# The second MLP's first product as seven block products, with weights' parts kept in HBM

## The chip, the cores and the metric

The kernel runs on one core of a Trainium2 chip. The metric is the device time of one execution in microseconds. Three runs of the kernel before gave 929.76, 930.53 and 929.92 us, so the median is 929.92. Profiles come from one profiled execution; its span runs from the first to the last instruction.

## The reference

Attention with random features over 4 batches, 8 heads, 576 tokens and head size 64 makes 2304 tokens of 512 values. Two MLPs follow, both 512 to 2048 to 512. All is float32.

```
attention: num = phi(q) (phi(k)^T v),  den = phi(q) sum(phi(k)),  x = num / (den + 1e-6)
first MLP:  h = x @ w_in;  g = max(h, 0) + alpha * min(h, 0);                       x = g @ w_out
second MLP: h = x @ w_in;  g = h if h >= 1, 0 if h <= -1, else (h + 1)^2 / 4;       out = g @ w_out
```

## The kernel before

**Split products.** To keep float32 precision each factor is split into a rounded part hi and a rest lo, and a product is three matmuls that add up in one PSUM bank (`mm3`, L257 to L260): hi hi, hi lo and lo hi. ScalarE makes hi (`hi_of`, L242, in some places VectorE), VectorE or GpSimd makes lo by a subtraction (`lo_of`, L250 to L253).

**Units.** The tokens stand in five blocks: four of 512 tokens (one of each batch) and one of 256 (the last 64 tokens of each). They form four groups, the last of which has a 512 and the 256 block. The 2048 features stand in 16 pieces of 128. A unit is one MLP, one group and one piece, so there are 2 x 4 x 16 = 128 units, and `mlps` (L813) runs them in order: h of the next unit (4 chunks of 128 input values, 3 matmuls each), then the second product of the unit before. h goes to one of two PSUM banks (h0, h1). `activate` turns it into g_hi and g_lo, and only then is the bank free. The second product adds into banks y0 to y3, a0 and a1 over all 16 pieces of a group. In the second MLP its result has the tokens on the partitions and goes straight to the output.

**Weights.** They arrive as 64-bit numbers; `convert` loads 128x1024 words (raw) and makes 128x512 float32 of them with two operations of ScalarE (or one of GpSimd), two of VectorE and one addition of GpSimd (L293). The converted weights of an MLP stay in SBUF. Each unit splits its two 128x512 pieces anew (`split_weight`: w_hi on ScalarE, w_lo on GpSimd), so every piece is split four times, once for each group.

**What sets the order.** All is written by a planner: each piece of work is a generator that asks for an engine and a time, a token (a buffer) or an event. `Plan.run` always takes the operation that can start first by its own table of costs (on a tie the one with the lower rank; `URGENT` is -10). So the order of each engine is fixed when the program is built, and the engines wait for each other by semaphores. All loads and stores are issued by SyncE's queue in that order. Attention is spread over the first three groups of the first MLP; when it ends (event "late"), the second MLP's weights are loaded.

Of the kernel before, what the change touches and what calls it, by code (L numbers as in the profile page):

```python
# [161 lines left out]
def favor_attention_two_mlps(  # L162
# [20 lines left out]
    nc = tc.nc  # L183
# [13 lines left out]
    NE = NF // 2  # L197
# [3 lines left out]
    WARM = 18  # L201
    COLS_NS = 1260
# [4 lines left out]
    wpool = ctx.enter_context(tc.tile_pool(name="w", bufs=NF))  # L207
# [5 lines left out]
    psum = ctx.enter_context(tc.tile_pool(name="psum", bufs=1, space=PSUM))  # L213

# [42 lines left out]
    def mm3(out_, wh, wl, mh, ml, first, last):  # L257
        nc.tensor.matmul(out_, wh, mh, start=first, stop=False)  # L258
        nc.tensor.matmul(out_, wh, ml, start=False, stop=False)  # L259
        nc.tensor.matmul(out_, wl, mh, start=False, stop=last)  # L260
# [39 lines left out]
    def load_weights(l, src):  # L300
        for f in range(NF):
            if l == 0:
                yield ev("unit", f - AHEAD)
            if l == 1 and f < NE:
                yield ev("late")
                w = late["pool"].tile([P, 2, DM], F32, tag="w", name="w2", bufs=NE)
            else:
                yield w_slots
                w = wpool.tile([P, 2, DM], F32, tag="w", name="w")
            weights[l, f] = w  # L310
            for a in range(2):
                i = l * len(groups) * NF + f
                plan.add(convert(w[:, a, :], src[f, :, a * 2 * DM : (a + 1) * 2 * DM], (l, f, a)), weight_rank(i))
# [4 lines left out]
    def split_weights(a):  # L318
        for i, (l, g, f) in enumerate(units):
            yield part_slots[a]  # L320
            yield ev("w", l, f, a)
            hi = parts_p.tile([P, DM], F32R, tag=f"wh{a}", name="w_hi")
            lo = parts_p.tile([P, DM], F32R, tag=f"wl{a}", name="w_lo")
            parts[i, a] = hi, lo
            plan.add(split_weight(a, i, weights[l, f][:, a, :], hi, lo), weight_rank(i) - 0.1)

    def split_weight(a, i, w, hi, lo):
# [4 lines left out]
        if l == 0 and g == len(groups) - 1:  # L332
            if ev("split", f).at is not None:
                plan.put(w_slots, 0)
            done("split", f)
# [348 lines left out]
    def attended():  # L684
# [6 lines left out]
        late["pool"] = ctx.enter_context(tc.tile_pool(name="late", bufs=1, reuse_waits="tile"))  # L691
# [10 lines left out]
    def split_x(l, b, c):  # L702
        n = sizes[b]
        k = b // B
        yield ev("x", l, b)
# [8 lines left out]
        done("xs", l, b, c)  # L714
# [5 lines left out]
    def activate(i, b, h, tag):  # L720
        l, _, f = units[i]
# [4 lines left out]
        if l == 0:  # L726
            a = alpha_sb[:, f : f + 1]
            yield _dve(n, lambda: nc.vector.tensor_scalar(tn, hn, 0.0, a, ALU.min, ALU.mult))  # L728
            yield _dve(n, lambda: nc.vector.scalar_tensor_tensor(hn, hn, 0.0, tn, ALU.max, ALU.add))
        else:  # L730

            yield _dve(n, lambda: nc.vector.tensor_scalar(tn, hn, -1.0, 1.0, ALU.max, ALU.min))  # L732
            yield _act(n, lambda: nc.scalar.activation(tn, tn, AF.Square, bias=half[:, 0:1], scale=0.5), 50)  # L733
            yield _dve(n, lambda: nc.vector.tensor_tensor(hn, hn, tn, ALU.max))  # L734
# [3 lines left out]
        g_hi = pool.tile([P, n], F32R, tag=f"gh{k}", name="g_hi", bufs=2)  # L738
        g_lo = pool.tile([P, n], F32R, tag=f"gl{k}", name="g_lo", bufs=2)
# [18 lines left out]
    def project(i, b, c, y):  # L758
        l, _, f = units[i]
# [5 lines left out]
        if l == 1:  # L765
            return _pe(mm3_ns(DM), lambda: mm3(y, gh[:, cc], gl[:, cc], hi, lo, first, last))
# [13 lines left out]
    def finish(l, b, c, y, tag, tokens):  # L780
        n = sizes[b]
        if l == 0:
# [12 lines left out]
        if l == 0:  # L795
            done("y", b, c)
            return
# [191 lines left out]
```

## Time and profile before

| | before |
|---|---|
| median of 3 runs | 929.92 us |
| span of the profiled execution | 928.7 us |
| TensorE busy | 914.9 us |
| VectorE, ScalarE, GpSimd busy | 543.0, 508.4, 456.0 us |
| moved by DMA | 53.41 MB |
| end of attention | about 321 us |
| second MLP's first matmul | about 526 us |
| last matmul starts | 923.3 us |

In the profile PE is TensorE's matmuls, PEld its weight loads, DVE VectorE, ACT ScalarE, POOL GpSimd, SP SyncE. Busy matmuls overlap: each has a latency behind its columns. How fast they follow each other is read from their starts.

### The profile page before, as it was taken

What the parts mean: (1) busy time and instruction counts of PE and PEld (TensorE: products, weight loads), DVE (VectorE), ACT (ScalarE), POOL (GpSimd) and SP (SyncE); (2) the same over time, 40 slices, a digit from 0 to 9 for tenths busy, and PEclk for the clock granted to TensorE, in tenths of its full rate; (3) what the DMA queues carried; (4) which work ended last, traced back from release to release, by engine and by line L of the source; (5) the groups of instructions that cost most, each with busy time, mean ns of one, the idle gap of its engine ahead of it and who ended that gap; (6) DMA issues with size and microseconds to landing.
All of it is one profiled execution on the core that took longest, in us unless ns stands there. A gap on an engine that the chain in (4) does not pass through costs nothing.

```text
span 928.7 us, 14192 instructions
## 1 busy us (share of the span) xinstructions
PE 914.9 (99%) x5244; PEld 759.3 (82%) x5244; DVE 543.0 (58%) x942; ACT 508.4 (55%) x1052; POOL 456.0 (49%) x375
## 2 busy tenths in 40 slices
PE   8899999999999999999999999999999999999997
PEld 7677887788888888888888888888888888888886
DVE  6988798866666678786544533353335355443332
ACT  7887777655556465665522544464445445443343
POOL 3656667543344477776643254444444444333330
PEclk9999999999999999999999999999999999999999
DMA  8654444111120022243200000010001000100002
GB/s 253 201 168 137 141 163 130 39 40 39 56 75 1 1 91 91 91 137 137 91 1 1 1 1 1 1 46 1 1 1 46 0 1 1 46 1 1 1 1 68
DMA packets 33861, 53.41 MB, mean 58 GB/s; under 512 B 20992, under 2 KB 21120, under 8 KB 33792
## 3 DMA queue, kind: packets, MB, share of 16 engines
q1 hardware_dynamic: 33712, 52.48, 17.6%
q8 instruction: 41, 0.67, 0.3%
q14 instruction: 28, 0.23, 0.1%
q10 hardware_dynamic: 80, 0.03, 0.0%
HBM read 47.78 MB, written 4.72 MB: 57 GB/s over the span
## 4 chain that ended last, share of the span: by engine, by line
PE 89%; DVE 5%; ACT 2%; DMA 1%; SPq 1%; issue 1%; POOL 0%; ACTq 0%; DVEq 0%
PE h L258 14%; PE h L260 13%; PE h L259 13%; PE y L258 12%; PE y L259 12%; PE y L260 12%; PE a L258 2%; PE a L260 2%; PE a L259 2%; PE a L394 2%; DMA raw<-w 1%; DVE x_lo L252 1%; PE a L431 1%; PE a L489 1%; DVE nm L361 1%
## 5 line engine op out<-in xcount | busy, mean ns | idle before, releaser
L253 POOL TENSOR_TENSOR w_lo<-w,w_hi 128x512 fp32r<-128x512 f32 x256 | 336.6, 1316 | 387.8 <-ACT w_hi L242 382.0
L242 ACT ACTIVATE w_hi<-w 128x512 fp32r<-128x512 f32 x256 | 161.7, 632 | 188.1 <-PE h L259 132.9
L258 PE MATMUL h<-x_hi,w_hi 128*128 128x512 f32 (+1 forms) x640 | 239.3, 374 | 0.0
L260 PE MATMUL h<-x_hi,w_lo 128*128 128x512 f32 (+1 forms) x640 | 236.0, 369 | 0.2 <-POOL w_lo L253 0.2
L259 PE MATMUL h<-x_lo,w_hi 128*128 128x512 f32 (+1 forms) x640 | 236.0, 369 | 0.0
L258 PEld LDWEIGHTS h<-x_hi,w_hi 128*128 128x128 f32 x640 | 120.7, 189 | 22.1 <-DVE g_lo L251 0.8
L260 PEld LDWEIGHTS h<-x_hi,w_lo 128*128 128x128 f32 x640 | 120.5, 188 | 21.2 <-POOL w_lo L253 0.7
L242 ACT ACTIVATE g_hi<-h 128x512 fp32r<-128x512 f32 (+1 forms) x160 | 88.8, 556 | 89.2 <-DVE h L734 46.7
L259 PEld LDWEIGHTS h<-x_lo,w_hi 128*128 128x128 f32 x640 | 120.7, 189 | 19.2
L251 DVE TENSOR_TENSOR g_lo<-h,g_hi 128x512 fp32r<-128x512 f32 (+1 forms) x160 | 100.6, 635 | 53.4 <-ACT g_hi L242 51.0
L732 DVE TENSOR_SCALAR t<-h 128x512 f32<-128x512 f32 x80 | 51.0, 637 | 131.6 <-PE h L260 129.9
L728 DVE TENSOR_SCALAR t<-h,alpha_sb 128x512 f32<-128x512 f32 x80 | 55.5, 694 | 87.9 <-PE h L260 86.7
L293 POOL TENSOR_TENSOR w<-w,raw 128x512 uint32<-128x512 uint32 x64 | 88.5, 1390 | 32.2 <-DVE w L292 26.5
L258 PE MATMUL y<-g_hi,w_hi 128*128 128x512 f32 x256 | 104.1, 407 | 0.0
L259 PE MATMUL y<-g_lo,w_hi 128*128 128x512 f32 x256 | 100.2, 391 | 0.0
L260 PE MATMUL y<-g_hi,w_lo 128*128 128x512 f32 x256 | 100.1, 391 | 0.0
L258 PE MATMUL y<-w_hi,g_hi 128*128 128x512 f32 x256 | 99.8, 390 | 0.0
L259 PE MATMUL y<-w_lo,g_hi 128*128 128x512 f32 x256 | 99.8, 390 | 0.0
L260 PE MATMUL y<-w_hi,g_lo 128*128 128x512 f32 x256 | 99.6, 389 | 0.0
L733 ACT ACTIVATE t<-t,half 128x512 f32<-128x512 f32 x80 | 54.5, 681 | 59.6 <-DVE t L732 59.6
L734 DVE TENSOR_TENSOR h<-h,t 128x512 f32<-128x512 f32 x80 | 51.4, 643 | 49.3 <-ACT t L733 49.3
L260 PEld LDWEIGHTS y<-g_hi,w_lo 128*128 128x128 f32 x256 | 48.1, 188 | 10.7
(121 smaller groups left out, 1262.6 us busy)
## 6 DMA issues: line engine op xcount, KB each, us to landing
raw<-w SPq DMA_DIRECT2D x64, 512.0 KB, 3.9
kq<-kq SPq DMA_DIRECT2D x15, 576.0 KB, 5.0
vm<-v SPq DMA_DIRECT2D x16, 256.0 KB, 3.6
out<-x SPq DMA_DIRECT2D x16, 256.0 KB, 2.0
vl<-v SPq DMA_DIRECT2D x32, 16.0 KB, 3.2
out<-x SPq DMA_DIRECT2D x4, 128.0 KB, 2.3
kq<-kq SPq DMA_DIRECT2D x1, 320.0 KB, 3.5
kq<-kq SPq DMA_DIRECT2D x1, 256.0 KB, 3.2
```

The lines of the kernel that those rows point to most:

```text
L242: ops = [_act(n, lambda: nc.scalar.activation(hi, src, AF.Copy))]
L251: "dve": _dve(n, lambda: nc.vector.tensor_tensor(*args), bias),
L253: "pool": _pool(n, lambda: nc.gpsimd.tensor_tensor(*args)),
L258: nc.tensor.matmul(out_, wh, mh, start=first, stop=False)
L259: nc.tensor.matmul(out_, wh, ml, start=False, stop=False)
L260: nc.tensor.matmul(out_, wl, mh, start=False, stop=last)
L293: yield _pool(n, lambda: nc.gpsimd.tensor_tensor(d, d, low, ALU.add))
L394: nc.tensor.matmul(o, x[rows, c], om[rows, :], start=True, stop=True)
L728: yield _dve(n, lambda: nc.vector.tensor_scalar(tn, hn, 0.0, a, ALU.min, ALU.mult))
L732: yield _dve(n, lambda: nc.vector.tensor_scalar(tn, hn, -1.0, 1.0, ALU.max, ALU.min))
L733: yield _act(n, lambda: nc.scalar.activation(tn, tn, AF.Square, bias=half[:, 0:1], scale=0.5), 50)
L734: yield _dve(n, lambda: nc.vector.tensor_tensor(hn, hn, tn, ALU.max))
```

## The change

The second MLP no longer runs in units. Its tokens form three groups of 768, each cut into two halves of 384; two feature pieces f = 2j and 2j + 1 form a pair j; the 512 input values are cut into two halves of 256. h of a pair is then a product of 2 x 2 blocks, made from seven block products in place of eight, with sums of blocks as factors:

```
s1 = a21 + a22   s2 = s1 - a11   s3 = a11 - a21   s4 = a12 - s2        (weights, once for each pair)
t1 = b12 - b11   t2 = b22 - t1   b22 - b12        b21 - t2             (inputs, once for each group)
products 0: a11 b11   1: a12 b21   2: s4 b22   3: a22 (b21 - t2)   4: s1 t1   5: s2 t2   6: s3 (b22 - b12)
u = p0 + p5;  h of the four corners: p0 + p1,  u + p4 + p2,  u + p6 + p3,  u + p4 + p6
```

A step is a group and a pair: 3 x 8 = 24 steps, each with 7 products of 2 chunks x 3 matmuls of 384 columns, in the order 0, 5, 1, 4, 6, 2, 3. Products 1, 2 and 3 go on adding in the bank of 0, 4 and 6, after ScalarE has copied that bank out (e0, e4, e6). VectorE adds u and makes the corners c1 and c2, ScalarE or VectorE copies c0, GpSimd makes the last corner of e4, e6 and u. The activation then works on these SBUF tiles (`corner`). The twelve sets of three matmuls of the second product of the step before stand between the seven products, in portions of 2, 1, 2, 2, 1, 2, 2.

The weights' sums, and hi and lo of all that the second MLP needs, are made once (`second_parts`, `keep`) after attention has ended, beside the first MLP's last group, and stored to HBM. Each step loads its three weight sets and two parts of w_out from there (`load_set`, `load_out`). The first MLP's weights stand in two pools of eight pieces, which are closed one after the other to make room for the split inputs. All tokens' x is one tile. The first MLP is computed as before.

```diff
+    ORDER = [0, 5, 1, 4, 6, 2, 3]
+    PIECES = [2, 1, 2, 2, 1, 2, 2]
+    w_sets = [[0, 1], [5, 4], [6, 2, 3]]
+    def keep(dst, src, key):
+        n = src.free_size()
+        yield stage_slots
+        both = late["pool"].tile([P, 2, n], F32R, tag="keep", name="w_keep", bufs=3)
+        hi, lo = both[:, 0, :], both[:, 1, :]
+        yield hi_of(hi, src, 600)
+        yield lo_of(lo, src, hi, ("pool", "dve2"), 400)
+        done("kept", *key)
+        plan.add(store_kept(dst, both, n, key), NU)
...
+    def load_set(s, k):
...
+        yield ev("stored", j, k)
...
+        yield set_slots[k]
...
+        yield _dma(P * n * 8, lambda: nc.sync.dma_start(both.bitcast(F32), kept[j, k]))
...
+    def inputs(p):
...
+        yield tt(t1, b12, b11, ALU.subtract)
+        yield tt(t2, b22, t1, ALU.subtract)
...
+        yield tt(b12, b22, b12, ALU.subtract)
...
+        yield tt(t2, b21, t2, ALU.subtract)
...
+    def added_corner(s, q, src, tag):
...
+        yield _dve(GH, lambda: nc.vector.tensor_tensor(e, src, u, ALU.add))
+        plan.put(h_banks, tag)
...
+    def corner(s, q, h, key):
...
+        yield _dve_fast(GH, lambda: nc.vector.tensor_scalar(t, h, -1.0, 1.0, ALU.max, ALU.min))
+        yield _act(GH, lambda: nc.scalar.activation(t, t, AF.Square, bias=half[:, 0:1], scale=0.5), 50)
+        yield _dve_two(GH, lambda: nc.vector.tensor_tensor(h, h, t, ALU.max))
...
+        yield hi_of(g_hi, h)
+        yield lo_of(g_lo, h, g_hi, ("dve2", "pool"), -300)
...
+    def product(s, i, o, first):
...
+            for c in range(K2):
+                r = slice((n * K2 + c) * P, (n * K2 + c + 1) * P)
+                mm3(o, hi[:, r], lo[:, r], xh[:, c, :], xl[:, c, :], first and c == 0, c == K2 - 1, not first)
...
+    def second_mlp():
...
+            for i, more in zip(ORDER, PIECES):
...
+                    yield product(s, i, o, chain is None)
...
+                for _ in range(more):
+                    yield from next(pieces, ())
```

The orders below come from the two programs as built. First TensorE in the second MLP, in the kernel before: the end of one unit's h (x_hi and x_lo are the input's parts, w_hi and w_lo the weight's) and the start of a second product.

```order
L260 MATMUL h_6076<-x_hi,w_lo 128x512
L258 MATMUL h_6076<-x_hi,w_hi 128x512
L259 MATMUL h_6076<-x_lo,w_hi 128x512
L260 MATMUL h_6076<-x_hi,w_lo 128x512
L258 MATMUL y_5969<-w_hi,g_hi 128x512
L259 MATMUL y_5969<-w_lo,g_hi 128x512
L260 MATMUL y_5969<-w_hi,g_lo 128x512
```

And in the changed kernel, inside a step: w_set is a loaded weight set with its hi and lo, w_out a loaded part of the second weight.

```order
L265 MATMUL h_7137<-x_hi,w_set 128x384
L266 MATMUL h_7137<-x_lo,w_set 128x384
L267 MATMUL h_7137<-x_hi,w_set 128x384
L265 MATMUL y_6097<-w_out,g_hi 128x512
L266 MATMUL y_6097<-w_out,g_hi 128x512
L267 MATMUL y_6097<-w_out,g_lo 128x512
L265 MATMUL y_6105<-w_out,g_hi 128x512
L266 MATMUL y_6105<-w_out,g_hi 128x512
L267 MATMUL y_6105<-w_out,g_lo 128x512
L265 MATMUL h_7165<-x_hi,w_set 128x384
```

Twelve matmuls of 512 columns to a bank of h became six of 384, and the second product, which stood in one piece behind them, is dealt out between them.

Next VectorE in the last group of the first MLP, in the kernel before: one unit's activation (t, then h with alpha, then g_lo for the 512 and the 256 block) and the start of the next.

```order
L728 TENSOR_SCALAR t_5604<-h0_5588,alpha_sb_80 128x512
L729 SCALAR_TENSOR_TENSOR h0_5588<-h0_5588,t_5604 128x512
L728 TENSOR_SCALAR t_5621<-h1_5603,alpha_sb_80 128x256
L729 SCALAR_TENSOR_TENSOR h1_5603<-h1_5603,t_5621 128x256
L251 TENSOR_TENSOR g_lo_5617<-h0_5588,g_hi_5616 128x512
L251 TENSOR_TENSOR g_lo_5634<-h1_5603,g_hi_5633 128x256
```

In the changed kernel, in the same group: x_133 is the tile of all tokens, x_sum a sum of its blocks, x_lo the rest of a split.

```order
L886 TENSOR_TENSOR x_133<-x_133 128x2x384
L259 TENSOR_TENSOR x_lo_5219<-x_sum_5139,x_hi_5218 128x768
L745 TENSOR_SCALAR t_5236<-h0_5212,alpha_sb_85 128x512
L259 TENSOR_TENSOR x_lo_5221<-x_133,x_hi_5220 128x768
L259 TENSOR_TENSOR x_lo_5223<-x_sum_5138,x_hi_5222 128x768
L886 TENSOR_TENSOR x_sum_5139<-x_133,x_sum_5139 128x768
L746 SCALAR_TENSOR_TENSOR h0_5212<-h0_5212,t_5236 128x512
L745 TENSOR_SCALAR t_5283<-h1_5235,alpha_sb_85 128x256
L746 SCALAR_TENSOR_TENSOR h1_5235<-h1_5235,t_5283 128x256
L258 TENSOR_TENSOR g_5282<-h0_5212,g_5282 128x512
L258 TENSOR_TENSOR g_5292<-h1_5235,g_5292 128x256
L295 SCALAR_TENSOR_TENSOR raw_5124<-raw_5124 128x512
```

Three operations of 768 columns came between the two halves of the activation of one bank, and conversions of the second MLP's weights stand behind it.

Last, VectorE where the second MLP passes from the first token group to the second, in the changed kernel (e, u and c are tiles of a step's block products).

```order
L1052 TENSOR_TENSOR c1_7102<-h0_7046,u_7014 128x384
L1075 TENSOR_SCALAR t_7113<-c1_7102 128x384
L259 TENSOR_TENSOR x_lo_7101<-x_133,x_hi_7100 128x768
L1052 TENSOR_TENSOR c2_7124<-h1_7075,u_7014 128x384
L1077 TENSOR_TENSOR c1_7102<-c1_7102,t_7113 128x384
L259 TENSOR_TENSOR x_lo_7123<-x_sum_5942,x_hi_7122 128x768
L1075 TENSOR_SCALAR t_7140<-e4_7056 128x384
L259 TENSOR_TENSOR g_lo_7142<-c1_7102,g_hi_7141 128x384
L886 TENSOR_TENSOR x_sum_7151<-x_133 128x768
L1077 TENSOR_TENSOR e4_7056<-e4_7056,t_7140 128x384
L886 TENSOR_TENSOR x_sum_7152<-x_133,x_sum_7151 128x768
```

The splits and sums of the next group's input stand among the corners of the last step of the group before.

## Rows read from the trace of the kernel before

**Rows 1.** page: span, busy time by engine, and the granted clock in 40 slices

```profile
span 928.7 us, 14192 instructions
...
PE 914.9 (99%) x5244; PEld 759.3 (82%) x5244; DVE 543.0 (58%) x942; ACT 508.4 (55%) x1052; POOL 456.0 (49%) x375
...
PEclk9999999999999999999999999999999999999999
```

**Rows 2.** windows, 530 to 770 us: busy us and instructions of each engine, clock, DMA

```profile
530.00:770.00 240.00, 240.00 (x1066) 198.93 (x1066) 105.12 (x152) 119.01 (x193) 113.42 (x88) 1.00 0.03 9
```

**Rows 3.** groups by line and form, TensorE into h: count, busy us, mean ns

```profile
L258 PE MATMUL h<-x_hi,w_hi 128*128 128x512 f32 x512 | 203.3, 397 | 0.0
...
L258 PE MATMUL h<-x_hi,w_hi 128*128 128x256 f32 x128 | 36.0, 282 | 0.0
```

**Rows 4.** order of time, TensorE: start us, duration us; 84 and 11 matmuls on

```profile
535.36 0.39 PE L258 MATMUL y<-w_hi,g_hi 128*128 128x512 f32 x1
...
554.40 0.39 PE L258 MATMUL h<-x_hi,w_hi 128*128 128x512 f32 x1
...
806.53 0.28 PE L258 MATMUL h<-x_hi,w_hi 128*128 128x256 f32 x1
...
807.84 0.28 PE L260 MATMUL h<-x_hi,w_lo 128*128 128x256 f32 x1
```

**Rows 5.** groups by line and form, other engines: count, busy us, mean ns, idle

```profile
L253 POOL TENSOR_TENSOR w_lo<-w,w_hi 128x512 fp32r<-128x512 f32 x256 | 336.6, 1316 | 387.8 <-ACT w_hi L242 382.0 <-PE y L260 2.8 <-PE h L260 1.8
...
L293 POOL TENSOR_TENSOR w<-w,raw 128x512 uint32<-128x512 uint32 x64 | 88.5, 1390 | 32.2 <-DVE w L292 26.5 <-POOL w_lo L253 1.6 <-PE a L260 1.6
L251 DVE TENSOR_TENSOR g_lo<-h,g_hi 128x512 fp32r<-128x512 f32 x128 | 88.2, 689 | 45.8 <-ACT g_hi L242 43.3
...
L252 DVE TENSOR_TENSOR x_lo<-x,x_hi 128x512 fp32r<-128x512 f32 x32 | 29.3, 956 | 6.1 <-ACT x_hi L242 6.1
...
L791 ACT COPY x<-y 128x512 f32<-128x512 f32 x24 | 13.9, 590 | 5.2 <-PE y L260 4.6
L251 DVE TENSOR_TENSOR g_lo<-h,g_hi 128x256 fp32r<-128x256 f32 x32 | 13.5, 421 | 7.6 <-ACT g_hi L242 7.6
...
L252 DVE TENSOR_TENSOR x_lo<-x,x_hi 128x256 fp32r<-128x256 f32 x8 | 3.9, 549 | 0.0
```

**Rows 6.** tile x_lo on VectorE: duration ns min/median/max, starts, forms

```profile
L252 DVE TENSOR_TENSOR x_lo<-x,x_hi x40: 405/678/1779, 50.2 to 787.4; 128x512 fp32r<-128x512 f32 x32, 128x256 fp32r<-128x256 f32 x8
```

**Rows 7.** one unit of the first MLP's last group, windows

```profile
461.78:470.14 8.36, 8.36 (x50) 7.38 (x49) 4.48 (x9) 2.25 (x4) 5.57 (x5) 1.00 0.00 0
```

**Rows 8.** windows, two early stretches full of loads: last two columns DMA share, GB/s

```profile
10.00:20.00 10.00, 9.01 (x135) 7.06 (x133) 9.12 (x21) 9.23 (x26) 3.32 (x4) 1.00 0.89 298
20.00:30.00 10.00, 9.72 (x122) 7.38 (x123) 9.37 (x20) 8.71 (x24) 7.77 (x8) 1.00 0.70 197
```

**Rows 9.** tile raw on SyncE's queue: 512 KB loads from issue to landing

```profile
DMA to landing us min/median/max: 3.4/3.9/8.7
```

**Rows 10.** order of time, the end

```profile
923.05 1.26 ACT L791 COPY x<-a 128x512 f32<-128x512 f32 x2
...
923.30 0.39 PE L260 MATMUL a<-w_hi,g_lo 128*128 128x512 f32 x1
923.66 2.44 SPq L805 DMA_DIRECT2D out<-x  x4
```

More of the change, by code (lines that the diff above doesn't have):

```diff
@@ L331, in split_weight @@
         done("part", i, a)
[L332 to L335, printed above, removed]
+        if i in (NU - NF // 2 - 1, NU - 1):
+            done("last split", i, a)
     free_banks = Tokens(["y0", "y1", "y2", "y3", "a0", "a1"])
@@ L868, in mlps @@
             plan.put(part_slots[1], 0)
+    ORDER = [0, 5, 1, 4, 6, 2, 3]
+    PIECES = [2, 1, 2, 2, 1, 2, 2]
+    NJ2 = NF // 2
+    STEPS = NG * NJ2
+    w_sets = [[0, 1], [5, 4], [6, 2, 3]]
+    place = {i: (k, n) for k, part in enumerate(w_sets) for n, i in enumerate(part)}
+    second, kept = {}, {}
+    w_of, out_of, x_of, g_of = {}, {}, {}, {}
+    set_slots = [*part_slots, Tokens([0])]
+    stage_slots = Tokens(range(3))
+    sum_slots = [Tokens([0]) for _ in range(2)]
+    x_slots = [Tokens([0]) for _ in range(7)]
@@ new lines, in favor_attention_two_mlps, with open_second @@
+    temp_slots = {k: Tokens([0]) for k in ("e0", "e4", "e6", "u", "c0", "c1", "c2", "t1", "t2")}
+    out_g_slots = [Tokens([0]) for _ in range(4)]
+    def open_second():
+        for k in range(2):
+            for a in range(2):
+                yield ev("last split", (NU - NF // 2 - 1, NU - 1)[k], a)
+            w_stacks[k].close()
+            name = ("second", "third")[k]
+            second[k] = ctx.enter_context(tc.tile_pool(name=name, bufs=1, side="right", reuse_waits="tile"))
+            done("second", k)
@@ new lines, in load_out @@
+    def load_out(s, u):
+        j = s % NJ2
+        if u:
+            yield ev("out part", s, 0)
+        elif s:
+            yield ev("out part", s - 1, 1)
+        yield ev("stored", j, 3 + u)
+        yield ev("first hidden")
+        yield g_slots[0]
+        both = moe_p.tile([P, 2, DM], F32R, tag="g0", name="w_out", bufs=2)
+        yield _dma(P * DM * 8, lambda: nc.sync.dma_start(both.bitcast(F32), kept[j, 3 + u]))
+        out_of[s, u] = both[:, 0, :], both[:, 1, :]
+        done("out part", s, u)
@@ new lines, in second_project, with piece @@
+    def second_project(s):
+        p, j = divmod(s, NJ2)
+        for u in range(2):
+            for r in range(NR):
+                yield piece(s, p, j, u, r)
+    ys2 = {}
+    def piece(s, p, j, u, r):
+        q = 2 * u + r // (NR // 2)
+        yield ev("out part", s, u)
+        yield ev("og", s, q)
+        tokens = y_banks if r < 4 else free_banks
+        if j == 0 and u == 0:
+            tag = yield tokens
+            ys2[r] = bank(tag), tag
+        y, tag = ys2[r]
+        hi, lo = out_of[s, u]
+        gh, gl = g_of[s, q]
+        cc = slice(r % (NR // 2) * P, (r % (NR // 2) + 1) * P)
+        first, last = j == 0 and u == 0, j == NJ2 - 1 and u == 1
+        yield _pe(mm3_ns(DM), lambda: mm3(y, gh[:, cc], gl[:, cc], hi, lo, first, last))
+        if last:
+            plan.add(store(p, r, y, tag, tokens), URGENT)
+        if r % (NR // 2) == NR // 2 - 1:
+            plan.put(out_g_slots[q], 0)
+        if r == NR - 1:
+            plan.put(g_slots[0], 0)
@@ L932, in favor_attention_two_mlps @@
     plan.add(attended(), 0)
-    for l in range(2):
-        plan.add(load_weights(l, (w1, w2)[l]), 0)
+    plan.add(load_weights(), 0)
+    for a in range(2):
+        plan.add(second_weights(a), 0)
     for a in range(2):
```

375 lines of the change are left out of this document (293 added, 82 removed).

## The prediction

> **What bounds the kernel now.** I read the busy times and the 40 slices first, then the windows, then the matmuls by form, then single rows in order of time. TensorE is busy 914.9 of 928.7 us and its granted clock is full in every slice [rows 1]. Busy time alone proves little, since a 512-column matmul shows 389 ns while the next one starts 227 ns later. The better sign is a long stretch without any gap: from 530 to 770 us, inside the second MLP, TensorE is busy 240.00 of 240.00 us while the other three lie near half (VectorE 105, ScalarE 119, GpSimd 113) [rows 2]. So nothing is waited for there, and the time of that stretch is the number of matmuls times their pitch. A change that takes matmuls away gives their time back in full, as long as the other engines and the transfers keep up with the shorter schedule. Those are the two sums below.
>
> **What goes: matmuls.** For both MLPs together each of the three lines of a split product has 512 matmuls of 512 columns and 128 of 256 columns into h [rows 3]. Half belong to the second MLP: 3 x 256 = 768 of 512 columns and 3 x 64 = 192 of 256. The pitch of 512 columns is (554.40 - 535.36) / 84 = 0.2267 us; that of 256 columns is (807.84 - 806.53) / 11 = 0.1191 us [rows 4]. The old first product therefore takes 768 x 0.2267 + 192 x 0.1191 = 174.1 + 22.9 = 197.0 us.
>
> In its place stand 24 steps (3 groups of 768 tokens, 8 pairs of 128 features) with 7 block products of 2 x 3 matmuls each: 1008 matmuls of 384 columns. No row has 384 columns. The bounds are the two pitches: 1008 x 0.1191 = 120 us (which would be fewer cycles than columns, so excluded by both rows: each is its columns at 2.4 GHz plus 12 to 13 ns) and 1008 x 0.2267 = 228.5 us (the price if 384 columns cost what 512 do). Since both known widths lie on one straight line, I take its middle, 0.1729 us, and get 174.3 us. That removes **22.7 us**. The second product keeps 864 matmuls of 512 columns, now 12 in a step in portions of one or two sets of three between the block products, as the order shows. Where the width changes in the old order, the first few matmuls come some ns late at most, so I charge nothing for the mixing and let the range hold 1 us for it.
>
> The order of TensorE is the same as before up to the last unit of the first MLP, so attention and most of the first MLP cost what they cost now. The tail also keeps its form: copy, then four stores after the last matmul, 923.30 to the span's end at 928.7 [rows 1, 10].
>
> **What is added beside it.** Nothing below runs on TensorE; it costs only where an engine falls behind. Prices: a VectorE operation with its operand in PSUM takes 689 ns for 512 and 421 ns for 256 columns; with both inputs in SBUF it takes 956 and 549 ns on average, while the median of all forty is 678 ns and the least 405; these two I read as 512 and 256 columns undisturbed [rows 5, 6]. A 768-column one, which no row has, is by the two lines 0.95 us undisturbed and 1.36 us at the average; I take 0.95 where GpSimd rests and the middle where it works. 384 columns come to 0.54 us.
>
> *A step of the second MLP.* VectorE has 15 operations of 384 columns, 15 x 0.54 = 8 us of a step of 42 x 0.1729 + 36 x 0.2267 = 15.4 us. ScalarE has 12, at about 0.5 us each, 6 us. GpSimd has two additions, near 2 us. All are below half to two thirds, and each eviction of a bank has 3 us (two or three sets of matmuls) until the bank is wanted. No stall.
>
> *The weights' parts.* Before, 128 splits of w_lo on GpSimd at 1316 ns and as many w_hi on ScalarE belonged to the second MLP; they go. Now each of 8 feature pairs gets four sums of 256 columns and five and a half 512-column splits once, in the last group of the first MLP. There a unit lasts 8.36 us (from one activation's start to the next) and VectorE works 4.48 us of it [rows 7], so there is room. But it is uneven. In the three units where also the first token group's input sums and their splits stand, I count from the order 3.5 us of activation each plus eight 768-column operations (8 x 0.95 = 7.6) plus conversions and weight splits: about 24.9 us in 25.1 us of TensorE, and 28.2 with the 768-column ones at their average price. In the second of these units three 768-column operations stand between the two halves of an activation, whose bank TensorE wants 12 x 0.2267 + 24 x 0.1191 = 5.6 us after it was filled; the activation alone takes some 3.5 us, and three more at 0.95 make 6.4. So between 0 and 3 us; I take 1.
>
> *The seam between the MLPs.* From the end of the last h1 to block product 4, which needs the bank that the shared sum u frees, TensorE has 12 x 0.2267 + 12 x 0.1191 of the unit before, as much again of the last unit, and three block products of 1.04 us: 11.4 us. On VectorE stand in this time, in order, two activation halves, three input splits, the two g_lo, three input sums, a conversion, three weight sums and u: 10.7 us undisturbed, 13.2 at the average price. In the first step no portion of the second product stands between the block products, so each copy of a bank has 1.04 us, and ScalarE has the six copies of the first MLP's results at 590 ns [rows 5] in the same queue. Last, the second weight set can only be asked for when the unit before has left its buffer, and is wanted 5.2 us later; a 512 KB load takes 3.9 us, at worst 8.7 [rows 9], and two more are in flight. These three waits overlap. Between 0.3 and 6 us; I take **2.5**.
>
> *The two changes of token group.* Between two u instructions VectorE has six splits, three sums and two casts of 768 columns besides the usual work, about 16.4 us for a step of 15.4, with a slack of some 2 us. Between 0 and 2.5 us each; I take 0.5 each, **1** in all.
>
> *The stream of weights.* Each step loads 0.5 + 0.5 + 0.75 + 2 x 0.5 MB = 2.88 MB, 187 GB/s. The nearest rows moved 298 GB/s at a DMA share of 0.89 and 197 GB/s at 0.70 [rows 8], which is 280 to 335 GB/s at full share, so the stream needs some 60%. The tightest load is the second part of w_out, asked for at the end of a step just after a 0.75 MB set and wanted 8.2 us later; both together are 1.3 MB, some 4.4 us of transfer beside the 2 us that a load spends otherwise. It holds, with 2 to 3 us to spare. I charge nothing; if the cover goes, each step pays.
>
> **The sum.** 928.7 - 22.7 + 1 + 2.5 + 1 = 910.5 us of span; the profiled execution's span is 1.2 us below the median of the runs, 929.9, and I keep that distance: **911.7 us**.
>
> A rule to weigh here: the change moves the activation's operands out of PSUM into SBUF, so 8 of the 15 operations of a step now have two SBUF inputs. The traced input splits of that kind range from 405 to 1779 ns with a median of 678 [rows 6], while g_lo, with one input in PSUM, stays at 689. The Trainium skill (SBUF — State Buffer, "Who interferes with whom") says that a VectorE instruction with two SBUF inputs and a GpSimd instruction that reads SBUF shut each other out for a whole instruction; by that rule the trace's spread is waiting for GpSimd. By it, two GpSimd additions would add at most some 2 us to VectorE's 8 in a step of 15.4, nothing on the path, but the preparation would go at the average price or above, which is the third case below.
>
> **The rivals.**
> *All hidden.* No stall outlasts its slack: 929.9 - 22.7 = 907.2 us, give or take 1 for the pitch. For it: not one gap in 240 us now [rows 2]. Against: VectorE is filled to the brim in three places.
> *VectorE bounds the preparation.* While GpSimd splits and converts, at 1316 and 1390 ns an operation [rows 5], every 768-column operation takes 1.36 us or more and the delays reach the activations: 3 us before the seam, 5 at it, 2.5 at each group change, 13 together, 920 us. For it: the 956 ns average [rows 5]. Against: the schedule sets the two engines' operations apart, and half of the old ones ran undisturbed.
> *The stream bounds each step* (the other side). All loads, preparatory stores and results stand in one in-order queue, and a store that waits for its data holds back every load behind it. It decides from the point where the 1.3 MB at a step's end need over 9.6 us, or a step's 2.88 MB over 15.4, that is below 187 GB/s; 197 was the lowest of the two busy rows. The gain is gone when each of 24 steps loses 22.7 / 24 = 0.95 us (176 GB/s); at 165 GB/s a step takes 17.5 us and the kernel 929.9 - 22.7 + 24 x 2.05 = 956 us. Against: loads of later steps are issued up to a step early.
> *384 columns go at the price of 512.* Then 228.5 - 197.0 = 31.5 us are added: 966 us. Both widths of [rows 4] speak against it; it goes into the same chance as the stream.
>
> **Chances.** The forecast's case, 909 to 914.5: 0.53. All hidden, 906 to 909: 0.16. VectorE bounds, 914.5 to 922: 0.22. A step loses just about the 0.95 us: 0.02. Slower: 0.07. A range from 906.5 to 919 leaves out about 0.2, the slower side and the worst of VectorE's case. What a measurement of this kernel can tell from no change is 0.2%, 1.9 us: faster 0.91, same 0.02, slower 0.07.
>
> **What would show it.** In the windows of a step between 560 and the end TensorE should be busy throughout, with starts of the 384-column matmuls 173 ns apart and one step every 15.4 us. Idle time of TensorE, if the forecast holds, lies at the seam near 530 us, released by VectorE or ScalarE, and in small pieces near 650 and 775 us. The DMA share in the second MLP should be near 0.6, and no h or y matmul should wait for a load after the first step. The forecast is wrong if matmuls wait for w_set or w_out in step after step, if the 384-column pitch is above 0.18 us, or if u or the corners' additions release TensorE in most steps.

## The result, and the profile after

The changed kernel takes 917.91 us (median of 4 runs, 917.28 to 921.34; the longest lies outside the range below) where the kernel before took 930.22 in the same session: a ratio of 0.9873 (95% interval 0.9854 to 0.9893), so 12.3 us faster where the prediction had 18. The forecast was 911.7 us in a range of 906.5 to 919. The time lies in the range, but not in its likeliest case (909 to 914.5): it lies in the band of the rival "VectorE bounds the preparation" (914.5 to 922, chance 0.22).

The page of the changed kernel: span, busy time, granted clock in 40 slices and the traffic of HBM (answers to [rows 1]).

```profile
span 916.3 us, 14599 instructions
...
PE 896.5 (98%) x5292; PEld 768.1 (84%) x5292; DVE 625.5 (68%) x1120; ACT 508.7 (56%) x1104; POOL 379.9 (41%) x327
...
PEclk9999999999999999999999999999999999999999
...
HBM read 116.99 MB, written 27.79 MB: 158 GB/s over the span
```

TensorE's 20 us that are not busy hide in the tenths of a slice. Windows of a few units show them. The columns are the busy us (and instructions) of PE, PEld, DVE, ACT and POOL, then the granted clock, the DMA share and GB/s. First two windows of the kernel before, then six of the changed one.

```profile
380.00:400.00 20.00, 20.00 (x94) 16.56 (x93) 17.11 (x28) 12.65 (x24) 14.81 (x11) 1.00 0.23 80
460.00:480.00 20.00, 20.00 (x118) 17.72 (x117) 9.30 (x17) 5.25 (x11) 9.93 (x8) 1.00 0.00 1
```

```profile
380.00:400.00 20.00, 18.51 (x86) 14.59 (x85) 18.03 (x23) 10.52 (x20) 13.36 (x10) 1.00 0.38 136
400.00:460.00 60.00, 60.00 (x340) 52.50 (x339) 46.67 (x78) 36.39 (x68) 47.23 (x38) 1.00 0.56 203
460.00:480.00 20.00, 16.71 (x89) 14.35 (x88) 18.10 (x23) 7.22 (x14) 9.92 (x7) 0.91 0.18 60
480.00:530.00 50.00, 50.00 (x290) 44.08 (x289) 44.36 (x71) 28.43 (x53) 36.41 (x28) 1.00 0.64 219
530.00:540.00 10.00, 8.56 (x52) 7.52 (x51) 9.99 (x12) 6.04 (x12) 4.05 (x3) 1.00 0.72 260
560.00:640.00 80.00, 80.00 (x404) 72.45 (x403) 41.03 (x85) 34.41 (x69) 12.93 (x12) 1.00 0.62 213
```

From 540 us to the last matmul TensorE has no gap, as before [rows 2]. The time is lost in three places ahead of that, and in each VectorE is busy for 9 tenths or more (at 460 us 18.10 of 20 us, where it was 9.30). In the second MLP the starts of its steps and of a run of 42 block matmuls show what a step costs: two step starts twenty steps apart, then the 384-column run up to the 512-column matmul behind it.

```profile
577.11 0.34 PE L265 MATMUL h<-x_hi,w_set 128*128 128x384 f32 x1
...
887.30 0.34 PE L265 MATMUL h<-x_hi,w_set 128*128 128x384 f32 x1
...
539.81 0.34 PE L265 MATMUL h<-x_hi,w_set 128*128 128x384 f32 x1
...
547.14 0.39 PE L265 MATMUL y<-w_out,g_hi 128*128 128x512 f32 x1
```

A step is 310.19 / 20 = 15.51 us and a 384-column matmul (547.14 - 539.81) / 42 = 0.1745 us. The second MLP's first product thus takes 1008 x 0.1745 = 175.9 us in place of 197.0, 21.1 less. Adding up, from the order of time, by how much each matmul starts later than the pitch of the matmul ahead of it allows, I find 9.3 us lost from 380 us on, and 0.5 in the same part of the kernel before. So -21.1 + 8.8 = -12.3 us, and the last matmul starts at 910.85 where it started at 923.30 [rows 10]: 12.45 earlier.

**The largest loss**, 5.1 us, is in the unit at 469 us. TensorE in order of time:

```profile
469.30 0.28 PE L267 MATMUL a<-g,w_parts 128*128 128x256 f32 x1
472.86 0.50 PE L265 MATMUL h<-x_hi,w_parts 128*128 128x512 f32 x1 [3.29 <-DVE g L258]
473.20 0.53 PE L266 MATMUL h<-x_lo,w_parts 128*128 128x512 f32 x1
473.53 0.63 PE L267 MATMUL h<-x_hi,w_parts 128*128 128x512 f32 x1
473.96 0.63 PE L265 MATMUL h<-x_hi,w_parts 128*128 128x512 f32 x1
...
476.52 0.49 PE L265 MATMUL h<-x_hi,w_parts 128*128 128x512 f32 x1
476.84 0.39 PE L266 MATMUL h<-x_lo,w_parts 128*128 128x512 f32 x1
```

The wait for the bank costs 3.4 us. Then seven starts follow 0.427 us apart (473.53 to 476.52), nearly twice the usual 0.2267: the lower of the clock's two levels (1.2 GHz), and the granted clock of the window is 0.91. That, with the late matmuls at its two ends, costs 1.7 us more. VectorE in the same time, then GpSimd:

```profile
461.31 0.95 DVE L886 TENSOR_TENSOR x_sum<-x,x_sum 128x768 f32<-128x768 f32 x1
462.18 2.05 DVE L886 TENSOR_TENSOR x<-x 128x768 f32<-128x768 f32 x1
464.15 1.49 DVE L259 TENSOR_TENSOR x_lo<-x_sum,x_hi 128x768 fp32r<-128x768 f32 x1
465.57 0.74 DVE L745 TENSOR_SCALAR t<-h,alpha_sb 128x512 f32<-128x512 f32 x1
466.23 0.94 DVE L259 TENSOR_TENSOR x_lo<-x,x_hi 128x768 fp32r<-128x768 f32 x1
467.09 2.05 DVE L259 TENSOR_TENSOR x_lo<-x_sum,x_hi 128x768 fp32r<-128x768 f32 x1
469.06 1.48 DVE L886 TENSOR_TENSOR x_sum<-x,x_sum 128x768 f32<-128x768 f32 x1
470.47 0.69 DVE L746 SCALAR_TENSOR_TENSOR h<-h,t 128x512 f32<-128x512 f32 x1
```

```profile
458.41 1.30 POOL L260 TENSOR_TENSOR w_parts<-w,w_parts 128x512 fp32r<-128x512 f32 x1 [0.34 <-ACT w_parts L249]
461.99 1.42 POOL L260 TENSOR_TENSOR w_parts<-w,w_parts 128x512 fp32r<-128x512 f32 x1 [2.28 <-ACT w_parts L249]
463.37 1.46 POOL L887 TENSOR_TENSOR w_sum<-w,w 128x256 f32<-128x256 f32 x1
466.21 2.11 POOL L260 TENSOR_TENSOR w_parts<-w,w_parts 128x512 fp32r<-128x512 f32 x1 [1.39 <-ACT w_parts L249]
468.29 1.45 POOL L887 TENSOR_TENSOR w_sum<-w,w_sum 128x256 f32<-128x256 f32 x1
```

Two things meet here. Three operations of the new preparation stand between t<-h and h<-h,t, the two halves of one activation, as the prediction read from the order. And five of the eight 768-column operations between 459 and 471 us take 1.45 to 2.05 us where the other three take 0.95 or 0.94. Each of the five began while a GpSimd operation ran, and each ends 0.82 us after that operation: the one at 462.18 ends at 464.23, GpSimd's split at 463.41. In the whole changed kernel this holds for every long one among its 33 additions and subtractions of 768 columns: nine, each ending 0.81 to 0.82 us behind GpSimd's. The one at 466.23 began together with a GpSimd split and took its usual 0.94; there the split took 2.11. So the two engines take turns, a whole operation at a time.

The long operations cost twice. Between the two halves they took 4.2 us, from 466.23 to 470.47. And the ones ahead of them hold back the first half: this h was complete at 463.99, but t<-h began only at 465.57, behind an operation of 2.05 and one of 1.49 us.

**The second loss**, 2.3 us, was not in the prediction: at 385 to 398 us the last token group of the first MLP begins, and its x_lo come late, so that two matmuls start 0.8 and 0.9 us late; the rest is small. In the kernel before these splits are long as well (two together 2.03, two 1.84 us), but the second pair begins at 392.50 there and at 395.06 here. The first of the two late starts:

```profile
394.76 0.39 PE L265 MATMUL h<-x_hi,w_parts 128*128 128x512 f32 x1
395.80 0.50 PE L266 MATMUL h<-x_lo,w_parts 128*128 128x512 f32 x1 [0.65 <-DVE x_lo L259]
```

**The third**, 1.7 us, is the seam, where three 768-column splits (2.14 us for two, 2.05 for one) stand ahead of g, the activation's low part:

```profile
534.72 0.50 PE L266 MATMUL y<-g,w_parts 128*128 128x512 f32 x1 [1.44 <-DVE g L258]
```

The two changes of token group (about 650 and 775 us) lose nothing.

### The profile page after: what moved, and what is told of

Same layout as the page of the kernel before. It is cut to its first block, busy times and chain, and to the rows that moved or that the text cites. A ratio compares the mean times of both kernels' runs of the same rounds, so it can differ in the third digit from the quotient of the medians.

```text
span 916.3 us, 14599 instructions
## 1 busy us (share of the span) xinstructions
PE 896.5 (98%) x5292; PEld 768.1 (84%) x5292; DVE 625.5 (68%) x1120; ACT 508.7 (56%) x1104; POOL 379.9 (41%) x327
## 4 chain that ended last, share of the span: by engine, by line
PE 82%; DVE 7%; ACT 4%; DMA 2%; issue 2%; POOL 1%; SPq 1%; ACTq 0%; DVEq 0%; POOLq 0%
PE h L265 12%; PE h L267 12%; PE h L266 12%; PE y L265 10%; PE y L267 10%; PE y L266 10%; PE a L265 4%; PE a L266 4%; PE a L267 4%; DMA raw<-w 2%; DVE x_lo L259 2%; PE a L412 2%; PE a L449 1%; PE a L507 1%; DVE t L745 1%
## 5 line engine op out<-in xcount | busy, mean ns | idle before, releaser
L260 POOL TENSOR_TENSOR w_parts<-w,w_parts 128x512 fp32r<-128x512 f32 x128 | 172.8, 1352 | 135.1 <-ACT w_parts L249 134.6
L265 PE MATMUL h<-x_hi,w_parts 128*128 128x512 f32 (+1 forms) x320 | 122.1, 382 | 3.3 <-DVE g L258 3.3
L266 PE MATMUL h<-x_lo,w_parts 128*128 128x512 f32 (+1 forms) x320 | 119.0, 372 | 1.4 <-DVE x_lo L259 1.4
L267 PE MATMUL h<-x_hi,w_parts 128*128 128x512 f32 (+1 forms) x320 | 118.8, 371 | 0.2 <-POOL w_parts L260 0.2
L249 ACT ACTIVATE w_parts<-w 128x512 fp32r<-128x512 f32 x128 | 80.9, 632 | 67.5 <-PE h L267 37.7
L265 PE MATMUL h<-x_hi,w_set 128*128 128x384 f32 x336 | 113.2, 337 | 0.0
L267 PE MATMUL h<-x_hi,w_set 128*128 128x384 f32 x336 | 112.9, 336 | 0.0
L266 PE MATMUL h<-x_lo,w_set 128*128 128x384 f32 x336 | 112.8, 336 | 0.0
L265 PE MATMUL y<-g,w_parts 128*128 128x512 f32 x256 | 104.1, 407 | 0.0
L266 PE MATMUL y<-g,w_parts 128*128 128x512 f32 x256 | 100.4, 392 | 1.5 <-DVE g L258 1.4
L267 PE MATMUL y<-g,w_parts 128*128 128x512 f32 x256 | 100.0, 391 | 0.0
L267 PE MATMUL y<-w_out,g_lo 128*128 128x512 f32 x192 | 75.2, 392 | 0.0
L265 PE MATMUL y<-w_out,g_hi 128*128 128x512 f32 x192 | 75.0, 391 | 0.0
L266 PE MATMUL y<-w_out,g_hi 128*128 128x512 f32 x192 | 74.7, 389 | 0.0
L265 PEld LDWEIGHTS h<-x_hi,w_parts 128*128 128x128 f32 x320 | 60.6, 190 | 14.4 <-DVE g L258 3.7
L267 PEld LDWEIGHTS h<-x_hi,w_parts 128*128 128x128 f32 x320 | 60.5, 189 | 11.2 <-POOL w_parts L260 0.7
```

What stands on the lines that cost most here:

```text
L249: ops = [_act(n, lambda: nc.scalar.activation(hi, src, AF.Copy))]
L260: "pool": _pool(n, lambda: nc.gpsimd.tensor_tensor(*args)),
L265: nc.tensor.matmul(out_, wh, mh, start=first, stop=False, skip_group_check=more)
L266: nc.tensor.matmul(out_, wh, ml, start=False, stop=False, skip_group_check=more)
L267: nc.tensor.matmul(out_, wl, mh, start=False, stop=last, skip_group_check=more)
```

## The experiments

Theories: **1, order** (preparation stands between halves of activations), **2, load** (VectorE has more to do there than fits, in any order), **3, GpSimd** (its operations lengthen VectorE's). All ratios are to the kernel before, measured beside each run; the changed kernel has 0.9873, and 0.001 is 0.93 us.

**The rank.**
```
-        r = URGENT + p
+        r = URGENT + 1 + p
```


> The input sums and splits of 768 columns get a rank behind the activations', so at an equal start an activation goes first; no work is added or removed. Theory 1 (order: the stalls come from 768-column operations that stand between the two halves of an activation): the wait of 3.3 us at 469.5 us, the 1.65 us of slow clock behind it and the 1.4 us at 533 us go, so 917.9 - 5 to 6.4 = 911.5 to 913 us (ratio to the kernel before 0.980 to 0.982). Theory 2 (load: VectorE has more work in these units than TensorE, whatever the order): the same 3 to 5 us of idle time turns up one to three units later or at the seam, 916 to 919 us. Theory 3 (GpSimd lengthens VectorE's operations): says nothing of the order; by it the 768-column operations still take 1.4 to 2.1 us wherever GpSimd adds or subtracts beside them, and 0.95 us where it rests.

Measured: 915.98 us, ratio 0.9830 (0.9817 to 0.9843), between the ranges of the two theories. One window, and the wait of that unit:

```profile
460.00:500.00 40.00, 39.46 (x229) 34.65 (x228) 36.47 (x52) 20.23 (x37) 26.55 (x21) 1.00 0.38 140
```

```profile
471.21 0.50 PE L265 MATMUL h<-x_hi,w_parts 128*128 128x512 f32 x1 [0.54 <-DVE g L258]
```

The same eight operations take as long as before (1.55, 0.95, 0.94, 2.05, 1.53, 1.44, 0.94, 2.06: 11.5 us against 11.4), but only one long one (1.53 us) now stands between the two halves: 3.29 us of waiting become 0.54, and the clock stays at 1.00. So order turned the long operations into this stall. Theory 2 has a small share at most: 2.1 us of late starts appear between 528 and 545 us, where there were 1.7, and the ratio's gain is 0.004, not 0.006.

**GpSimd writes constants** in place of its subtractions and sums of weights and results.
```
-            "pool": _pool(n, lambda: nc.gpsimd.tensor_tensor(*args)),
+            "pool": _pool(n, lambda: nc.gpsimd.memset(lo.bitcast(F32), 0.001)),
...
-            "pool": lambda: _pool(n, lambda: getattr(nc.gpsimd, fn)(*args)),
+            "pool": lambda: _pool(n, lambda: nc.gpsimd.memset(args[0], 0.01)),
```


> Every low part that GpSimd subtracts (both MLPs' weights) and every sum that it adds (weights' sums, two additions of a step) is written by GpSimd as a constant instead, so the results are not the reference's; the order of the instructions on TensorE, VectorE, ScalarE and the queues is the same, and VectorE's own work is untouched. Theory 3 (VectorE's operations with both operands in SBUF are lengthened by GpSimd's operations with two SBUF operands): all eight 768-column operations near 460 to 470 us take 0.95 us in place of 0.95 to 2.05, which takes 3.8 us from that row of eight; the wait of 3.3 us and the slow clock behind it go, the seam's 1.4 us shrinks below 0.5, the group start at 394 us loses its 1.9 us: 910 to 912 us (ratio 0.978 to 0.981). Theories 1 and 2 without it (the operations are long for another reason, as the loads' writes into SBUF or the matmuls' reads): they stay at 1.4 to 2.05 us and the time stays at 917 to 918.5 us.

Measured: 908.92 us, ratio 0.9757 (0.9744 to 0.9770), just below the expected range. VectorE's operations of that unit, in the changed kernel's order:

```profile
461.84 0.75 DVE L745 TENSOR_SCALAR t<-h,alpha_sb 128x512 f32<-128x512 f32 x1 [0.39 <-PE h L267]
462.51 0.95 DVE L259 TENSOR_TENSOR x_lo<-x,x_hi 128x768 fp32r<-128x768 f32 x1
463.37 0.95 DVE L259 TENSOR_TENSOR x_lo<-x_sum,x_hi 128x768 fp32r<-128x768 f32 x1
464.24 0.95 DVE L886 TENSOR_TENSOR x_sum<-x,x_sum 128x768 f32<-128x768 f32 x1
465.11 0.69 DVE L746 SCALAR_TENSOR_TENSOR h<-h,t 128x512 f32<-128x512 f32 x1
```

All eight take 0.95 or 0.96 us (7.6 in all, 3.8 less), the six near the seam 0.95, the four 512-column x_lo of the last group 0.69 in place of 1.19 on average, and the time lost from 380 us on falls from 9.3 to 1.6 us. Theory 3 is shown. The order alone, with three operations between the halves, costs next to nothing while they take 0.95 us each (0.4 us lost from 455 to 480 us, where it was 5.2): the stall needs both. The constants also take less time (0.53 us against 1.35), but a shorter GpSimd is not the reason: the x_lo at 463.37 began together with one of GpSimd's constants and still took 0.95, so it is not any operation of GpSimd that lengthens. The Trainium skill (SBUF — State Buffer, "Who interferes with whom") states just this: two SBUF inputs on VectorE contend with a GpSimd instruction that reads SBUF, not with one that only writes it. The traces agree: nine operations are long beside reading ones in the changed kernel, none of the 33 here.

**Later preparation**, alone and with the rank.
```
     def second_weights(a):
         yield ev("late")
+        yield ev("last group")
...
+            if g == len(groups) - 1 and f == 0:
+                done("last group")
```


> The preparation of the second MLP's weights waits for the second product of the first MLP's last group to begin, about 75 us later than in the changed kernel; nothing else is edited. All theories: the 1.9 us lost at 394 to 399 us, where the splits of the last group's input stand beside weight preparation, goes. Theory 1 (order): the stall near 470 us stays as it is, 3.3 + 1.65 us, total 917.9 - 1.9 = 916.0 us. Theory 2 (load): the same work must fit in less time, so the idle time of TensorE between 460 us and the first steps of the second MLP grows by more than was saved, 919 to 925 us, and the first steps wait for weights that are not stored yet.

> Both edits together: input sums and splits ranked behind the activations, and the weights' preparation begun only with the last group's second product. Theory 1 (order): all three stalls go, 917.9 - 1.9 - 5 - 1.4 = 909.5 to 911 us. Theory 2 (load): no better than the rank alone, or worse, 916 to 923 us, since what is taken from the group's start is missing before the seam.

Measured: 927.84 us, ratio 0.9957 (0.9945 to 0.9970), and with the rank 932.85, ratio 1.0027 (1.0013 to 1.0041): nearly all of the gain gone, then all of it, and both worse than any theory had it. The group's start is clean in both (TensorE busy 20.00 of 20.00 from 380 to 400), as every theory had it. But at 460 us TensorE waits 6.09 us in the first, where four 768-column operations in a row stand ahead of g: order again, 7.9 us lost there in place of 5.2. And in both the preparation runs on into the second MLP, where 9.4 us are lost from 525 us on in the first and 21 in the second, in place of 1.8. With the rank, SyncE's queue in order of time, its waits from 630 to 665 us (us in total, times, longest), and TensorE:

```profile
651.26 0.32 SPq L940 DMA_DIRECT2D w_out<-w_keep  x1
...
654.14 0.32 SPq L970 DMA_DIRECT2D w_out<-w_out  x1
```

```profile
SPq L970 <- DMA w_out<-w_keep: 10.9, 3, 5.4
SPq L940 <- DVE w_keep L259: 7.3, 3, 4.0
```

```profile
659.48 0.77 PE L265 MATMUL y<-w_out,g_hi 128*128 128x512 f32 x1 [11.92 <-DMA w_out<-w_out]
```

A part of w_out is stored at 651.26 us only, since the store waits for VectorE's w_keep; the load waits for a store to land and is issued at 654.14; TensorE waits 11.92 us for it. So theory 2 has its place: 75 us less of room cost 8 us by the ratios, and 18 with the rank. How much of that is VectorE's load (in the changed kernel it was already busy 44.36 of the 50 us from 480 to 530) and how much the way through HBM and the one queue, no run separates.

**Eight products, parts kept.** Core of the edit: no sums of weights, inputs or results, each corner two chained products.
```
-    ORDER = [0, 5, 1, 4, 6, 2, 3]
...
+    ORDER = [0, 1, 2, 3, 4, 5, 6, 7]
...
-    w_sets = [[0, 1], [5, 4], [6, 2, 3]]
...
+    w_sets = [[0, 1], [4, 5]]
```


> The first product of the second MLP as eight block products of 384 columns (no sums of inputs, weights or results; each half of a feature block over each half of the tokens is two chained products), with the weights' parts still made once and kept in HBM and the groups of 768 tokens kept. It separates the two halves of the change. By the pitch 0.1745 us the product takes 24 x 48 x 0.1745 = 201.0 us against 197.0 of the kernel before and 175.9 of the changed one. Theory (TensorE sets every step, and the gain is the seventh product's alone): 917.9 + 25.1 = 943.0 us less what the sums cost at the group start, near 470 us and at the seam, up to 8 us: 935 to 943 us, slower than the kernel before by 0.5 to 1.4%. Rival (keeping the parts in HBM gains time of its own, since VectorE, ScalarE and GpSimd lose their splits): below 930 us.

**Six products.** Product 1 is left out, all else is kept.
```
+        if i == 1:
+            return _pe(10, lambda: None)
         return _pe(K2 * mm3_ns(GH), products)
```


> Product 1 of the seven is left out (its bank keeps product 0 alone, so results are wrong), with all loads, sums and activations kept: a step has 36 matmuls of 384 and 36 of 512 columns. It asks how much shorter a step could get before another engine or the stream decides. Theory (TensorE sets the step with room to spare on the others): a step of 15.51 - 6 x 0.1745 = 14.46 us, total 917.9 - 25.1 = 892.8 us, give or take 1. Rival (VectorE or the stream of weights is just below its limit at 15.5 us): a step stays above 14.8 us and the time above 900 us, with TensorE waiting for VectorE or for w_set and w_out.

Measured: eight, 938.55 us, ratio 1.0079 (1.0064 to 1.0095); six, 896.67 us, ratio 0.9635 (0.9614 to 0.9656). Two neighbouring step starts of each, eight first:

```profile
576.26 0.34 PE L265 MATMUL h<-x_hi,w_set 128*128 128x384 f32 x1
...
592.80 0.34 PE L265 MATMUL h<-x_hi,w_set 128*128 128x384 f32 x1
```

```profile
576.49 0.34 PE L265 MATMUL h<-x_hi,w_set 128*128 128x384 f32 x1
...
590.95 0.34 PE L265 MATMUL h<-x_hi,w_set 128*128 128x384 f32 x1
```

Steps of 16.54, 15.51 and 14.46 us for eight, seven and six: 1.04 us for each product, its six matmuls at 0.1745. So TensorE alone sets the step, with at least 1 us to spare on the others, and the whole gain is the missing eighth product's: with eight, keeping the parts makes the kernel slower than before. Six gave 22.1 us by the ratios, not the 25.1 of 24 steps, and missed its expectation by 3 to 4: its first two steps stay nearly as long as they were (0.9 us lost in each), and the steps at the changes of token group lose 0.4 and 0.8.

**More traffic.** Each load of a part of w_out, from the third step on, issued twice, then three times.
```
+        for _ in range(1 if s > 1 else 0):
+            extra = stage_p.tile([P, 2 * DM], U32, tag="raw", name="extra", bufs=RAWS)
+            yield _dma(P * DM * 8, lambda: nc.sync.dma_start(extra, ...))
```


> From the third step on each load of a part of w_out is issued a second time, into a buffer that nothing reads: 1.05 MB more per step, 3.9 to 4.1 MB in 15.5 us, some 260 GB/s in place of 195. Theory (the stream has room): the steps stay at 15.5 us and the time at 917 to 919 us. Rival (the queue's order and its share of 0.55 to 0.7 already hold loads back at the tight places): matmuls wait for w_out in step after step, 0.5 us or more each, 928 us or more.

> As the run before with each load of w_out issued three times, two of them into buffers that nothing reads: 2.1 MB more per step, about 5.1 MB in 15.5 us, 330 GB/s, as much as the busiest 20 us of the changed kernel moved (327 GB/s at a share of 0.95). By the theory that the stream has room up to some 330 GB/s this is the edge: the step grows to 15.5 to 17 us, the time is 918 to 950 us, and where it grows, matmuls wait for w_set or w_out. By the rival, which already sees a loss with one more load, it is above 950 us.

Measured: 923.28 us, ratio 0.9907 (0.9881 to 0.9932), and 928.22, ratio 0.9972 (0.9952 to 0.9993). A window of the first, one of the second, and where the first loses time:

```profile
560.00:640.00 80.00, 80.00 (x404) 72.55 (x403) 40.89 (x84) 34.16 (x67) 13.97 (x13) 1.00 0.81 281
```

```profile
560.00:640.00 80.00, 80.00 (x404) 72.32 (x403) 41.23 (x85) 34.15 (x67) 12.93 (x12) 1.00 0.92 328
```

```profile
682.37 0.47 PE L265 MATMUL y<-w_out,g_hi 128*128 128x512 f32 x1 [1.76 <-DMA w_out<-w_out]
```

At 281 and even 328 GB/s TensorE is busy throughout and a step takes 15.51 us. The first time lies between its two theories, the second in its range, but both expectations missed the place: the loss is in the steps after the changes of token group, where the results' six stores stand in the same queue (17.5 and 16.9 us with one more load, up to 19.7 with two; with two, one wait of 1.26 us for VectorE's u comes on top). So the stream has some 100 GB/s to spare in the middle of a group and little at its changes.

**Splits moved from GpSimd to VectorE.** With the rank, low parts of the first MLP's weights may go to VectorE: in its last group (20 of 32), everywhere (78 of 128), or without a handicap (109; there the input sums and splits also come behind the first weights' preparation).
```
-        yield lo_of(lo, w, hi, ("pool",))
+        yield lo_of(lo, w, hi, ("pool", "dve2") if g == len(groups) - 1 else ("pool",), 400)
```


> The rank of the first run (input sums and splits behind the activations), and in the first MLP's last group the low parts of its weights may go to VectorE in place of GpSimd: where the planner finds VectorE free 400 ns earlier it puts them there (20 of 32). A low part of 512 columns is about 0.68 us of VectorE alone; on GpSimd it is 1.3 us, during which a VectorE operation with two SBUF operands waits. If the lengthening by GpSimd is what is left of the stalls, the 5.7 us of idle time that the rank alone left between 380 us and the end fall to 2 to 4 us: 912 to 914.5 us by the runs' scale where the rank alone had a ratio of 0.983, so 0.979 to 0.9815. If VectorE is simply overfull there, its added 20 x 0.68 = 13.6 us push the activations back and the ratio is 0.983 to 0.990.

> As the run before, with that choice in all of the first MLP (76 of the low parts of its weights then go to VectorE, 42 stay). If attention, which also uses VectorE heavily, bears it, the gain at the last group is the same and the start of the second MLP comes up to 2 us earlier: ratio 0.977 to 0.981. If the added 76 x 0.68 = 52 us reach attention's chain, the first 270 us grow by 2 us or more and the ratio is 0.983 to 0.99.

> As the run before with no handicap for VectorE (108 low parts there, 19 on GpSimd), and the input sums and splits ranked behind the first weights' preparation too. More is moved off GpSimd, so less lengthening, but VectorE is fuller: ratio 0.977 to 0.981 if the lengthening decides, 0.983 or more if VectorE's own load does, with stalls spread over the first 530 us.

Measured: 0.9847 (0.9834 to 0.9860), 0.9831 (0.9814 to 0.9848), 0.9880 (0.9861 to 0.9899). None beats the rank alone. Waits of 1.3 to 1.6 us for g remain at 400, 461 and 471 us in the first of them, which has four long 768-column operations there in place of five; that VectorE's own added work takes the place of the lengthening is likely, not shown.

**A pause**, with the rank.
```
         for f in range(NF):
+            if f >= 5:
+                yield ev("xs", B - 1, KC - 1)
             yield w2_slots[a]
```


> The rank of the first run, and from the sixth weight on the preparation pauses until the last group's 512-column tokens are split (x_lo near 394 to 399 us), so that less of it lies beside these splits; it is not put off for the 75 us of the later start. If the lengthening of x_lo by GpSimd's preparation is the cause of the 1.8 us lost there, that loss goes and the ratio falls from 0.983 to 0.9805 to 0.982. If the sum of work before the seam decides, as with the later start, the 1.8 us and more come back as idle time between 400 and 560 us: 0.983 to 0.986.

Measured: 913.31 us, ratio 0.9812 (0.9798 to 0.9827), inside the first of the two expected ranges. The x_lo at the group's start (the first of the three still takes 1.67 us):

```profile
389.80 2.87 DVE L259 TENSOR_TENSOR x_lo<-x,x_hi 128x512 fp32r<-128x512 f32 x3
...
393.97 0.68 DVE L259 TENSOR_TENSOR x_lo<-x,x_hi 128x512 fp32r<-128x512 f32 x1
```

The four are done at 394.65 in place of 397.47, TensorE is busy 20.00 of 20.00 us from 380 to 400, and 4.4 us are lost from 380 us on in place of 9.3. The pause keeps all of the preparation away, VectorE's share with GpSimd's, so it doesn't tell the two apart; the constants gave a clean start too (20.00 of 20.00), with the preparation in place. This is the best version found, faster than the kernel before and than the changed one (their intervals don't meet); against the rank alone its interval overlaps.

## Why the prediction was right in sign and off in size

The range held with 1.1 us to spare, and partly by luck: 911.7 + 1.6 (matmuls) + 4.1 (the three units) + 2.3 (the group's start) - 0.8 (the seam) - 1 (the changes of group) = 917.9. One term lay outside its own bounds, one was missing, and two that came out smaller paid for part of it.

*Bound by TensorE; the gain is matmuls times pitch.* Shown: steps of 14.46, 15.51 and 16.54 us for six, seven and eight products.

*Matmuls removed, -22.7.* It was -21.1. The interpolated 0.1729 us was 0.1745, so a step takes 15.51 us and not 15.42.

*The weights' parts and the three units, +1 (0 to 3).* This step failed: it cost 5.1. The place and the mechanism (three operations between two halves of an activation) were right. The price was not: the sum took 0.95 us each, while two of the three took 2.05 and 1.48 beside GpSimd; it let the activation start as soon as its bank was full, while two long operations ahead held it back by 1.6; and it left out that TensorE then runs at the lower level, 1.7 us. The undisturbed 0.95 itself was exact. The average price of 1.36 fits the row of eight (10.9 us, measured 11.4), but not the single operations that stand in the way. The trace of the kernel before could have told: 13 of its 32 x_lo splits of 512 columns were long, each ending 0.54 to 0.55 us after the GpSimd operation that ran when it began. A row of minimum, median and maximum hides that.

*The start of the last token group.* No term: 2.3 us. The window I took as a sample of the room [rows 7] lies some 65 us behind it. The preparation's operations stand among that group's splits too; the pause and the constants both make the start clean.

*The seam, +2.5 (0.3 to 6).* 1.7. TensorE waited for g of the last unit behind the three splits, not for the bank that u frees, and the first loads were not late.

*The changes of token group, +1.* Nothing lost: GpSimd, with little but its two additions a step, is busy 8.7 of 60 us from 640 to 700 us, so the 768-column operations fit; one at each change still took 1.72 us behind a GpSimd addition.

*The stream, 0.* Right. Its rival needed a queue that delivers less than 187 GB/s, and 328 GB/s still held the step. In the sum behind it the spare of the tightest load is 8.2 - 4.4 - 2 = 1.8 us, not 2 to 3, and the 9.6 us are given without their working; the term doesn't change by either. Its mechanism is there: from 380 to 540 us the changed kernel's queue waits 28.5 us for GpSimd's w_keep and 20.1 for VectorE's. But no matmul of the changed kernel from 380 us on waited for a load; where the preparation was put off, one waited 11.92 us.

*The rivals.* Of "VectorE bounds the preparation" the mechanism and the first two places came true: 5.1 us in place of 3 before the seam, 1.7 in place of 5 at it, 8.8 in place of 13 in all, with the group's start for the changes of group. I gave the forecast's case 0.53 and this one 0.22, because half of the old splits had run undisturbed; but GpSimd was to be busiest just where the new operations went.

## What to carry to other kernels

Where TensorE bounds a kernel, matmuls taken away come back in full in the steady part; ask instead where the work that replaces them is done, and price it there with the neighbours that it will have, not at the average. Rank preparation behind anything that frees a bank, since an operation between two halves of an eviction adds its whole length to it, and a wait for GpSimd with it. And don't begin such preparation late to clear one place: here the room lost cost 8 to 18 us, the stall 2.3.

## What was not expected of the hardware

VectorE's operations with two inputs in SBUF don't slow down beside GpSimd's reading ones, they wait: a long one of 768 columns ends 0.82 us after GpSimd's operation (nine of nine in the changed kernel), a long x_lo of 512 columns 0.55 us after it (13 of 13 in the kernel before). So its price is what GpSimd still has to run, plus that.

After 3.29 us without a matmul the granted clock fell to its lower level for about 3 us, at a cost of half the wait; after waits of 1.44 and 0.54 us only the first matmul was some 0.1 us late. What decides it these runs don't settle: with the later preparation it fell after a wait of 1.76 us as well, which one of 0.38 followed, and with eight products after 2.28 us (0.83 from 397 to 407 us), but with the later preparation and the rank it stayed at 1.00 after 2.35 us. And 328 GB/s in one in-order queue hid behind TensorE for 80 us without a single late load.
